# Causal attention ahead of two MLP blocks on one core: PSUM banks as separate tiles, and another order of scores, transposes and copies

## Chip, core and metric

One core of a Trainium2 chip (trn2) runs the whole program in one launch. The metric is the device time of that launch in microseconds (us). Times inside an execution come from a hardware profile of one execution: start and duration of each instruction on each engine, counted from the start of the span. The engines are TensorE (PE in the profile; its weight loads are listed apart as PEld), VectorE (DVE), ScalarE (ACT), GpSimd (POOL) and SyncE (SP), which here only issues DMAs.

## What is computed

Two batches, 12 heads, 448 positions, head size 64, all fp32. The causal attention output, laid out as 896 rows of 768, goes through two MLP blocks one after the other (768 to 2048 to 768, with a parametric ReLU in the first and a clipped square in the second).

```python
scores = scale * np.matmul(q, k.transpose(0, 1, 3, 2))
scores = np.where(mask, -1000000000.0, scores)          # causal
scores = scores - np.max(scores, axis=-1, keepdims=True)
attn = np.exp(scores)
attn = attn / (np.sum(attn, axis=-1, keepdims=True) + 1e-09)
x = np.matmul(attn, v)                                  # then (B*S, H*D)
h = x @ w_in;  g = np.maximum(h, 0) + alpha * np.minimum(h, 0);  x = g @ w_out
h = x @ w2_in; g = where(h >= 1, h, where(h <= -1, 0, (h + 1)**2 / 4)); out = g @ w2_out
```

## The kernel before

The program has two stages. The attention stage (lines 463 to 526) loops over 12 pairs of heads, `for p in range(NP + 2)`. The MLP stage (`run_layer`, lines 280 to 311) then runs four layers of matmuls of 128x448 columns back to back.

A pair holds two heads j = 0 and 1 on the two halves of 64 partitions. The 448 query rows are three row tiles i = 0, 1, 2 of 128 rows and a rest of 64 rows (i = NQ = 3); a row tile needs keys up to its own end, so the score tiles have 128, 256, 384 and 448 columns. The rests of the two heads are done together in one matmul with a block-diagonal `qdiag`.

Three pairs are in work at once. In turn p of the loop, in program order: `scores` of pair p for row tiles 0 and 1, then the rest (lines 493, 494); `expo` (ScalarE); `attnv` of pair p-2 and its evacuation `high` on ScalarE (lines 497 to 499); `spare(0)`, which from turn 3 on issues one step of the splitting of an MLP weight; `scores` for row tile 2; `transp` of pair p-1 (lines 504, 511, 512); `low` on VectorE; `expo` for row tile 2; `norm` of pair p (GpSimd and one reciprocal on VectorE); the DMA loads for later pairs, issued by SyncE. The last two turns have no new pair and take in the first MLP matmuls (`fill`) instead.

Each engine takes its instructions in that program order; the schedule is fixed by hand, and the framework adds the waits. It orders accesses per tile of a pool: an engine that writes a PSUM tile waits for readers of the same tile on another engine, and a reader waits for the last write into the tile ahead of it.

The PSUM has eight banks of 512 fp32 columns. Before, tag `s` is one tile of two banks (head j in bank j), `rest` and `o` one bank each, and tag `t` two buffers of two banks.

In `scores` (lines 366 to 394) every score matmul is followed at once by its masked reduction on VectorE (line 390), which writes the masked scores to SBUF and the row minimum of the negated scores to `stat`. In `transp` (lines 415 to 440) 64x64 blocks of the probabilities go through TensorE transposes into a `t` tile, partition half h of the rows into bank h; then line 440 copies them to `pt` in SBUF, head 0 by ScalarE and head 1 by VectorE, each copy reading both banks. There are three calls a pair: row tile 0 with the rest, row tile 1, row tile 2. In `attnv` (lines 442 to 450) eight products, four key chunks c by two heads j, add up in the bank `o`, over columns c*128 to 448; the heads fill the two column halves of the array. An fp32 matmul appears as two instructions in the profile, a transpose as one.

`evac_out` (lines 220 to 229) ends the program; the last two output tiles come from one two-bank `t` tile.

Of the kernel before, what the change touches and what calls it, by code (L numbers as in the profile page):

```python
# [22 lines left out]
def attention_moe_moe_kernel(ctx: ExitStack, tc: tile.TileContext, qk, v, w1, w2, w3, w4, alpha, out):  # L23
# [8 lines left out]
    nc = tc.nc  # L32
# [205 lines left out]
    def new_banks():  # L238

        def one(pool, tag):  # L240
            return pool.tile([128, 512], F32, tag=tag, name="ps")

        def two(pool, tag):
            both = pool.tile([128, 1024], F32, tag=tag, name="ps")
            return both[:, :512], both[:, 512:]

        while True:
            yield from two(ps_s, "s")
            yield one(ps_o, "rest")
            yield one(ps_o, "o")  # L250
            yield from two(ps_t, "t")
            yield from two(ps_t, "t")
# [61 lines left out]
    class Attention:  # L314
# [51 lines left out]
        def scores(self, p, tiles):  # L366
# [4 lines left out]
            if NQ in tiles:  # L371
                both = self.ps_o.tile([128, 512], F32, tag="rest", name="rest_ps")
            else:
                both = self.ps_s.tile([128, 1024], F32, tag="s", name="s_ps")
            off = 0
            for i in tiles:
                for n, (e, col) in enumerate(self.rows(p, i)):
                    w = e.shape[1]
                    ps = both[:, n * 512 + off:n * 512 + off + w]
                    if i == NQ:  # L380
                        nc.tensor.matmul(ps, lhsT=self.qdiag[p % 3], rhs=t[:, 1, :], start=True, stop=True)  # L381
                        m = mask_rest
                    else:
# [4 lines left out]
                        m = mask[:, REST - w:]  # L388

                    nc.vector.tensor_tensor_reduce(  # L390
                        out=e, in0=ps, in1=m, scale=-SCALE, scalar=3.0e38, op0=ALU.add, op1=ALU.min,
                        accum_out=self.st[p][:, 0, col:col + 1],
                    )
                off += w
# [10 lines left out]
        def norm(self, p):  # L405
# [3 lines left out]
            for i in (0, NQ, 1, 2):  # L409
# [5 lines left out]
        def transp(self, p, tiles):  # L415

            ps = self.ps_t.tile([128, 1024], F32, tag="t", name="t_ps").rearrange("p (h n) -> p h n", h=2)
            if 0 in tiles:
                self.pt[p] = self.ap.tile([Q, 2, NC, S], F32, tag="pt", name="pt", bufs=2)
            pt, off, copies = self.pt[p], 0, []  # L420
            for i in tiles:
                n = NC if i == NQ else i + 1
                rows = self.rows(p, i)
                dst = ps[:, :, off:off + len(rows) * n * D].rearrange("p h (j c q) -> p h j c q", c=n, q=D)
                off += len(rows) * n * D
                for c in range(n):
                    for j, (e, _) in enumerate(rows):
                        e = self.prest[p % 3] if i == NQ else e
                        for h in range(2):
                            g = slice(h * D, (h + 1) * D)  # L430
                            nc.tensor.transpose(dst[:, h, j, c, :], e[g, c * Q:(c + 1) * Q], ident[g, g])  # L431
                for j, copy in enumerate((nc.scalar.copy, nc.vector.tensor_copy)):
# [23 lines left out]
    with tc.manual_schedule():  # L456
# [6 lines left out]
        with ExitStack() as pa:  # L463
# [18 lines left out]
            for p in range(NP + 2):  # L482
# [20 lines left out]
                if mid:  # L503
                    at.transp(p - 1, (0, NQ))
# [74 lines left out]
```

## Time and profile before

| | us |
|---|---|
| median of 3 runs | 684.62 (677.09 to 686.32) |
| the profiled execution, its own time | 675.95 |
| its span in the profile | 674.1 |
| TensorE busy (matmuls) | 617.2 |
| VectorE busy | 424.7 |
| ScalarE busy | 248.0 |
| GpSimd busy | 132.6 |
| mean granted TensorE clock, share of 2.4 GHz | 0.932 |

The busy times are sums over both stages and must be read stage by stage. The attention stage runs from about 9 us to about 209 us, the MLP stage from there to the end. "Idle before" and the arrow in a row tell how long the engine stood still ahead of the group and what released it. Matmul ends are modelled, and a matmul's duration includes its latency, so rows that follow each other at once overlap a little.

### The profile page before, as it was taken

What the parts mean: (1) busy time and instruction counts of PE and PEld (TensorE: products, weight loads), DVE (VectorE), ACT (ScalarE), POOL (GpSimd) and SP (SyncE); (2) the same over time, 40 slices, a digit from 0 to 9 for tenths busy, and PEclk for the clock granted to TensorE, in tenths of its full rate; (3) what the DMA queues carried; (4) which work ended last, traced back from release to release, by engine and by line L of the source; (5) the groups of instructions that cost most, each with busy time, mean ns of one, the idle gap of its engine ahead of it and who ended that gap; (6) DMA issues with size and microseconds to landing.
All of it is one profiled execution on the core that took longest, in us unless ns stands there. A gap on an engine that the chain in (4) does not pass through costs nothing.

```text
span 674.1 us, 8430 instructions
## 1 busy us (share of the span) xinstructions
PE 617.2 (92%) x3057; PEld 505.8 (75%) x3057; DVE 424.7 (63%) x797; ACT 248.0 (37%) x509; POOL 132.6 (20%) x179
## 2 busy tenths in 40 slices
PE   7776677777789999999999999999999999999997
PEld 3333333333367999999999999999999999999996
DVE  1333333433336889889886666688888986666650
ACT  2344333434322433433333232345556453322220
POOL 1222322222220333343300000024334331000000
PEclk9996776777779999999999999999999999999999
DMA  4421111310002333332344333423323224534430
GB/s 125 142 69 50 53 45 44 90 44 0 1 1 94 97 137 94 99 121 63 109 142 125 93 100 113 163 94 128 107 95 108 96 63 124 153 122 131 141 93 27
DMA packets 25673, 62.29 MB, mean 92 GB/s; under 512 B 5280, under 2 KB 13984, under 8 KB 25632
## 3 DMA queue, kind: packets, MB, share of 16 engines
q1 hardware_dynamic: 23760, 60.15, 28.8%
q10 hardware_dynamic: 1872, 1.61, 0.7%
q8 instruction: 24, 0.39, 0.2%
q14 instruction: 17, 0.14, 0.1%
HBM read 58.99 MB, written 2.75 MB: 92 GB/s over the span
## 4 chain that ended last, share of the span: by engine, by line
PE 89%; DVE 6%; ACT 3%; issue 1%; POOL 0%; ACTq 0%; DVEq 0%; POOLq 0%
PE ps L262 69%; PE s_ps L385 9%; PE o_ps L447 5%; PE rest_ps L381 3%; DVE pexp L390 3%; DVE pt L440 2%; ACT pt L440 2%; PE t_ps L431 2%; ACT pexp L400 2%; PE warm_ps L72 1%; DVE stat L408 0%; DVE stat L390 0%; DVE w_split L153 0%; DVE w_f L147 0%; ACT w_split L150 0%
## 5 line engine op out<-in xcount | busy, mean ns | idle before, releaser
L262 PE MATMUL ps<-x,w_split 128*128 128x448 f32 x1152 | 235.2, 366 | 0.7 <-DVE w_split L153 0.7
L262 PE MATMUL ps<-g,w_split 128*128 128x448 f32 x1152 | 234.1, 365 | 0.9 <-DVE o_sb L226 0.9
L262 PEld LDWEIGHTS ps<-g,w_split 128*128 128x128 f32 x1152 | 216.3, 188 | 18.3 <-DVE o_sb L226 1.3
L262 PEld LDWEIGHTS ps<-x,w_split 128*128 128x128 f32 x1152 | 216.2, 188 | 18.4 <-DVE w_split L153 1.1
L177 POOL TENSOR_TENSOR g<-act_g,g 128x448 fp32r<-128x448 f32 x64 | 85.5, 1336 | 275.3 <-ACT g L176 275.2
L150 ACT CAST w_split<-w_f 128x512 fp32r<-128x512 f32 (+1 forms) x80 | 56.6, 707 | 127.4 <-DVE w_f L147 96.7
L385 PE MATMUL s_ps<-qk_raw 64*128 64x128 f32 (+2 forms) x144 | 70.6, 584 | 33.3 <-DVE stat L390 33.3
L153 DVE TENSOR_TENSOR w_split<-w_f,w_split 128x512 fp32r<-128x512 f32 (+1 forms) x80 | 66.0, 825 | 49.2 <-ACT w_split L150 49.0
L390 DVE CUSTOM_DVE_ANT_0 pexp<-s_ps,mask 128x128 f32<-128x128 f32 (+2 forms) x72 | 30.0, 417 | 94.3 <-PE s_ps L385 94.3
L385 PEld LDWEIGHTS s_ps<-qk_raw 64*128 64x128 f32 x144 | 30.7, 265 | 61.7 <-DVE stat L390 57.9
L176 ACT CAST g<-act_g 128x448 fp32r<-128x448 f32 x64 | 36.2, 565 | 76.5 <-DVE act_g L189 62.8
L147 DVE SCALAR_TENSOR_TENSOR w_f<-w_raw,w_f 128x512 uint32<-128x512 uint32 (+1 forms) x80 | 63.4, 793 | 1.4
L141 DVE SCALAR_TENSOR_TENSOR w_f<-w_raw,w_f 128x512 uint32<-128x512 uint32 (+1 forms) x80 | 63.4, 793 | 1.4
L129 DVE TENSOR_SCALAR w_f<-w_f 128x512 f32<-128x512 f32 (+1 forms) x80 | 58.2, 727 | 9.5 <-ACT w_f L113 9.3
L113 ACT ACTIVATE w_f<-w_raw 128x512 f32<-128x512 f32 (+1 forms) x80 | 61.2, 765 | 1.3 <-DMA w_raw<-w 1.3
L400 ACT ACTIVATE pexp<-pexp,stat 128x128 f32<-128x128 f32 (+2 forms) x72 | 36.4, 506 | 57.3 <-DVE stat L390 57.3
L447 PEld LDWEIGHTS o_ps<-pt,v 128*64 128x64 f32 x192 | 18.5, 192 | 30.8 <-issue 14.3
L135 DVE TENSOR_SCALAR w_f<-w_f 128x512 uint32<-128x512 uint32 (+1 forms) x80 | 38.0, 475 | 1.4
L447 PE MATMUL o_ps<-pt,v 128*64 128x320 f32 (+3 forms) x192 | 37.2, 544 | 0.6 <-ACT pt L440 0.6
L411 POOL TENSOR_SCALAR pexp<-pexp,stat 128x128 f32<-128x128 f32 (+2 forms) x72 | 33.8, 486 | 13.6 <-DVE stat L390 9.6
L431 PE MATMUL t_ps<-ident,pexp 64*128 64x64 f32 x288 | 21.2, 241 | 15.5 <-DVE pt L440 15.5
L201 ACT ACTIVATE act_t<-act_t,half 128x448 f32<-128x448 f32 x32 | 21.5, 672 | 37.7 <-DVE act_t L200 37.7
(43 smaller groups left out, 286.3 us busy)
## 6 DMA issues: line engine op xcount, KB each, us to landing
w_raw<-w SPq DMA_DIRECT2D x32, 768.0 KB, 4.3
w_raw<-w SPq DMA_DIRECT2D x48, 512.0 KB, 3.7
qk_raw<-qk SPq DMA_DIRECT2D x11, 448.0 KB, 3.6
out<-o_sb SPq DMA_DIRECT2D x12, 112.0 KB, 1.7
out<-o_sb ACTq DMA_DIRECT2D x12, 112.0 KB, 1.7
v<-v SPq DMA_DIRECT2D x12, 56.0 KB, 2.5
v<-v SPq DMA_DIRECT2D x12, 48.0 KB, 2.0
v<-v SPq DMA_DIRECT2D x12, 40.0 KB, 1.9
```

What stands on the lines that cost most here:

```text
L113: nc.scalar.activation(out=f32(w), in_=f32(hi), func=AF.Abs)
L129: nc.vector.tensor_scalar(out=f32(w), in0=f32(w), scalar1=HI_MIN, scalar2=HI_MAX, op0=ALU.max, op1=ALU.min)
L141: nc.vector.scalar_tensor_tensor(out=w, in0=hi, scalar=0xC0000000, in1=w, op0=ALU.bitwise_and, op1=ALU.bitwise_or)
L147: nc.vector.scalar_tensor_tensor(out=w, in0=lo, scalar=29, in1=w, op0=ALU.logical_shift_right, op1=ALU.bitwise_or)
L150: nc.scalar.copy(s[:, 0, :n], f32(w))
L153: nc.vector.tensor_sub(s[:, 1, :n], f32(w), f32(s[:, 0, :n]))
L177: nc.gpsimd.tensor_sub(t[:, 1, :], g, f32(t[:, 0, :]))
L262: nc.tensor.matmul(ps[b][:, :S], lhsT=ws[:, part, k * 128:(k + 1) * 128], rhs=src[b, kk][:, xp, :], start=first and part == 0 and xp == 0, ...
L385: nc.tensor.matmul(ps, lhsT=t[h, 0, i * Q:(i + 1) * Q], rhs=t[h, 1, :w], start=True, stop=True)
L390: nc.vector.tensor_tensor_reduce(out=e, in0=ps, in1=m, scale=-SCALE, scalar=3.0e38, op0=ALU.add, op1=ALU.min, accum_out=self.st[p][:, 0, c ...
L400: nc.scalar.activation(out=e, in_=e, func=AF.Exp, bias=st[:, 0, col:col + 1], scale=-1.0, accum_out=st[:, 1, col:col + 1],)
L447: nc.tensor.matmul(ps[j * D:(j + 1) * D, c * Q:S], lhsT=vraw[:, c, j, :], rhs=pt[:, j, c, c * Q:S], start=c == 0, stop=c == NC - 1,)
```

## The change

PSUM is cut into single-bank tiles: `s0`, `s1` (head 0 and 1 of the row tiles), `s2` (the rest), `o`, and two buffers each of `t0` and `t1`. `new_banks` hands the MLP stage the same eight banks one by one. `scores` issues all matmuls of a call first and all reductions after them. `transp` puts partition half h into the tile `t{h}`; for row tiles ScalarE copies all of half 0 and VectorE all of half 1 (both heads in one copy), into separate ranges of `pt`; the rest gets its own tile `pt_rest`, and both its copies are VectorE's. The calls are now (0, 1), (NQ), (2). `attnv` does the 384 columns of the row tiles in six products, chunk by head, whose moving operand and output are two interleaved sets of runs of 64 columns, and the rest's 64 columns in eight products of their own. `norm` scales row tile 1 ahead of the rest.

```diff
--- before.py
+++ after.py
@@ -237,19 +237,10 @@
 
     def new_banks():
 
-        def one(pool, tag):
-            return pool.tile([128, 512], F32, tag=tag, name="ps")
-
-        def two(pool, tag):
-            both = pool.tile([128, 1024], F32, tag=tag, name="ps")
-            return both[:, :512], both[:, 512:]
-
+        pools = (ps_s, "s0"), (ps_s, "s1"), (ps_s, "s2"), (ps_o, "o"), (ps_t, "t0"), (ps_t, "t1"), (ps_t, "t0"), (ps_t, "t1")
         while True:
-            yield from two(ps_s, "s")
-            yield one(ps_o, "rest")
-            yield one(ps_o, "o")
-            yield from two(ps_t, "t")
-            yield from two(ps_t, "t")
+            for pool, tag in pools:
+                yield pool.tile([128, 512], F32, tag=tag, name="ps")
 
     def new_tile():
         return next(banks)
@@ -369,29 +360,30 @@
                 self.st[p] = self.ap.tile([Q, 2, 2 * NQ + 1], F32, tag="stat", name="stat", bufs=4)
             t = self.raw[p]
             if NQ in tiles:
-                both = self.ps_o.tile([128, 512], F32, tag="rest", name="rest_ps")
+                banks = [self.ps_s.tile([128, 512], F32, tag="s2", name="rest_ps")]
             else:
-                both = self.ps_s.tile([128, 1024], F32, tag="s", name="s_ps")
-            off = 0
+                banks = [self.ps_s.tile([128, 512], F32, tag=f"s{j}", name=f"s{j}_ps") for j in range(2)]
+            off, todo = 0, []
             for i in tiles:
                 for n, (e, col) in enumerate(self.rows(p, i)):
                     w = e.shape[1]
-                    ps = both[:, n * 512 + off:n * 512 + off + w]
+                    ps = banks[n][:, off:off + w]
                     if i == NQ:
                         nc.tensor.matmul(ps, lhsT=self.qdiag[p % 3], rhs=t[:, 1, :], start=True, stop=True)
-                        m = mask_rest
+                        todo.append((e, ps, mask_rest, col))
                     else:
                         h = slice(n * D, (n + 1) * D)
                         nc.tensor.matmul(
                             ps, lhsT=t[h, 0, i * Q:(i + 1) * Q], rhs=t[h, 1, :w], start=True, stop=True
                         )
-                        m = mask[:, REST - w:]
-
-                    nc.vector.tensor_tensor_reduce(
-                        out=e, in0=ps, in1=m, scale=-SCALE, scalar=3.0e38, op0=ALU.add, op1=ALU.min,
-                        accum_out=self.st[p][:, 0, col:col + 1],
-                    )
+                        todo.append((e, ps, mask[:, REST - w:], col))
                 off += w
+
+            for e, ps, m, col in todo:
+                nc.vector.tensor_tensor_reduce(
+                    out=e, in0=ps, in1=m, scale=-SCALE, scalar=3.0e38, op0=ALU.add, op1=ALU.min,
+                    accum_out=self.st[p][:, 0, col:col + 1],
+                )
 
         def expo(self, p, tiles):
             st = self.st[p]
@@ -406,7 +398,7 @@
             sums = self.st[p][:, 1]
             nc.gpsimd.tensor_scalar_add(sums, sums, 1e-9)
             nc.vector.reciprocal(sums, sums)
-            for i in (0, NQ, 1, 2):
+            for i in (0, 1, NQ, 2):
                 for e, col in self.rows(p, i):
                     nc.gpsimd.tensor_scalar(
                         out=e, in0=e, scalar1=sums[:, col:col + 1], scalar2=1.0, op0=ALU.mult, op1=ALU.mult
@@ -414,38 +406,53 @@
 
         def transp(self, p, tiles):
 
-            ps = self.ps_t.tile([128, 1024], F32, tag="t", name="t_ps").rearrange("p (h n) -> p h n", h=2)
+
+            ps = [self.ps_t.tile([128, 512], F32, tag=f"t{h}", name=f"t{h}_ps") for h in range(2)]
             if 0 in tiles:
-                self.pt[p] = self.ap.tile([Q, 2, NC, S], F32, tag="pt", name="pt", bufs=2)
-            pt, off, copies = self.pt[p], 0, []
+
+                self.pt[p] = (
+                    self.ap.tile([Q, 2, 2, NQ, NQ * D], F32, tag="pt", name="pt", bufs=2),
+                    self.ap.tile([Q, 2, NC, D], F32, tag="pt_rest", name="pt_rest", bufs=2),
+                )
+            (pt, pt_rest), off, copies = self.pt[p], 0, []
             for i in tiles:
                 n = NC if i == NQ else i + 1
                 rows = self.rows(p, i)
-                dst = ps[:, :, off:off + len(rows) * n * D].rearrange("p h (j c q) -> p h j c q", c=n, q=D)
+                dst = [
+                    t[:, off:off + len(rows) * n * D].rearrange("p (j c q) -> p j c q", c=n, q=D) for t in ps
+                ]
                 off += len(rows) * n * D
                 for c in range(n):
                     for j, (e, _) in enumerate(rows):
                         e = self.prest[p % 3] if i == NQ else e
                         for h in range(2):
                             g = slice(h * D, (h + 1) * D)
-                            nc.tensor.transpose(dst[:, h, j, c, :], e[g, c * Q:(c + 1) * Q], ident[g, g])
-                for j, copy in enumerate((nc.scalar.copy, nc.vector.tensor_copy)):
-                    to = pt[:, j, :n, i * Q:]
-                    if i == NQ:
-
-                        copies.append((copy, to, dst[:, j, 0]))
-                    else:
-                        copies.append((copy, to[:, :, :Q].rearrange("p c (h q) -> p h c q", h=2), dst[:, :, j]))
+                            nc.tensor.transpose(dst[h][:, j, c, :], e[g, c * Q:(c + 1) * Q], ident[g, g])
+                if i == NQ:
+
+                    for h in range(2):
+                        copies.append((nc.vector.tensor_copy, pt_rest[:, h], dst[h][:, 0]))
+                else:
+                    for h, copy in enumerate((nc.scalar.copy, nc.vector.tensor_copy)):
+                        copies.append((copy, pt[:, h, :, :n, i * D:(i + 1) * D], dst[h]))
             for copy, to, src in copies:
                 copy(to, src)
 
         def attnv(self, p):
-            ps = self.o[p] = self.ps_o.tile([2 * D, 512], F32, tag="o", name="o_ps")
-            pt, vraw = self.pt[p], self.vraw[p % 5]
+            o = self.o[p] = self.ps_o.tile([2 * D, 512], F32, tag="o", name="o_ps")
+            (pt, pt_rest), vraw = self.pt[p], self.vraw[p % 5]
+            for c in range(NQ):
+                for j in range(2):
+                    nc.tensor.matmul(
+                        o[j * D:(j + 1) * D, c * Q:REST].rearrange("p (i h q) -> p h i q", h=2, q=D),
+                        lhsT=vraw[:, c, j, :],
+                        rhs=pt[:, :, j, c, c * D:].rearrange("p h (i q) -> p h i q", q=D),
+                        start=c == 0, stop=c == NQ - 1,
+                    )
             for c in range(NC):
                 for j in range(2):
                     nc.tensor.matmul(
-                        ps[j * D:(j + 1) * D, c * Q:S], lhsT=vraw[:, c, j, :], rhs=pt[:, j, c, c * Q:S],
+                        o[j * D:(j + 1) * D, REST:S], lhsT=vraw[:, c, j, :], rhs=pt_rest[:, j, c, :],
                         start=c == 0, stop=c == NC - 1,
                     )
 
@@ -501,14 +508,14 @@
                 if new:
                     at.scores(p, (2,))
                 if mid:
-                    at.transp(p - 1, (0, NQ))
+                    at.transp(p - 1, (0, 1))
                 if old:
                     low()
                 if new:
                     at.expo(p, (2,))
                 spare(2)
                 if mid:
-                    at.transp(p - 1, (1,))
+                    at.transp(p - 1, (NQ,))
                     at.transp(p - 1, (2,))
                 if new:
                     at.norm(p)
```

## Rows read from the trace of the kernel before

**Rows 1.** The page, granted TensorE clock in 40 slices, tenths of full speed
```profile
PEclk9996776777779999999999999999999999999999
```

**Rows 2.** Busy time by stretch: window, length, engines' busy us, PEclk, DMA share, GB/s
```profile
90.00:120.00 30.00, 21.71 (x121) 11.60 (x118) 11.03 (x39) 10.90 (x36) 7.20 (x16) 0.67 0.17 49
120.00:150.00 30.00, 21.32 (x124) 10.52 (x122) 12.12 (x42) 12.65 (x39) 7.20 (x16) 0.73 0.25 75
...
280.00:300.00 20.00, 20.00 (x101) 18.53 (x100) 18.38 (x26) 6.24 (x11) 6.65 (x6) 1.00 0.31 112
```

**Rows 3.** Timeline, TensorE, first group of turns 0, 1, 3, 12: start, us, what
```profile
9.41 0.79 PE L385 MATMUL s_ps<-qk_raw 64*128 64x128 f32 x2
...
21.19 0.79 PE L385 MATMUL s_ps<-qk_raw 64*128 64x128 f32 x2 [0.66 <-DVE stat L390]
...
50.26 0.44 PE L385 MATMUL s_ps<-qk_raw 64*128 64x128 f32 x2
...
193.04 4.27 PE L447 MATMUL o_ps<-pt,v 128*64 128x448 f32 x16 [0.57 <-ACT pt L440]
```

**Rows 4.** Timeline, TensorE's matmuls of turn 6, without the transposes
```profile
97.02 0.44 PE L385 MATMUL s_ps<-qk_raw 64*128 64x128 f32 x2
98.78 0.79 PE L385 MATMUL s_ps<-qk_raw 64*128 64x128 f32 x2 [1.32 <-DVE stat L390]
99.97 1.22 PE L385 MATMUL s_ps<-qk_raw 64*128 64x256 f32 x2 [0.39 <-DVE stat L390]
101.71 1.22 PE L385 MATMUL s_ps<-qk_raw 64*128 64x256 f32 x2 [0.53 <-DVE stat L390]
102.86 1.86 PE L381 MATMUL rest_ps<-qk_raw,qdiag 128*128 128x448 f32 x2
104.65 3.68 PE L447 MATMUL o_ps<-pt,v 128*64 128x448 f32 x16
108.26 1.19 PE L385 MATMUL s_ps<-qk_raw 64*128 64x384 f32 x2
110.11 0.59 PE L385 MATMUL s_ps<-qk_raw 64*128 64x384 f32 x1 [0.66 <-DVE stat L390]
...
113.74 0.74 PE L385 MATMUL s_ps<-qk_raw 64*128 64x128 f32 x2
```

**Rows 5.** Timeline, turn 6: first reduction of row tile 2, copies, last transposes
```profile
109.48 0.56 DVE L390 CUSTOM_DVE_ANT_0 pexp<-s_ps,mask 128x384 f32<-128x384 f32 x1 [3.23 <-PE s_ps L385]
...
111.47 0.27 ACT L440 COPY pt<-t_ps 128x128 f32<-128x128 f32 x1 [2.56 <-PE t_ps L431]
...
111.77 0.29 DVE L440 COPY pt<-t_ps 128x128 f32<-128x128 f32 x1 [0.15 <-ACT pt L440]
112.10 0.37 ACT L440 COPY pt<-t_ps 128x256 f32<-128x256 f32 x1 [0.36 <-DVE pt L440]
...
112.50 0.42 DVE L440 COPY pt<-t_ps 128x256 f32<-128x256 f32 x1 [0.44 <-ACT pt L440]
...
113.07 0.90 PE L431 MATMUL t_ps<-ident,pexp 64*128 64x64 f32 x12 [1.44 <-DVE pt L440]
```

**Rows 6.** Busy time by stretch, single microseconds of turn 6
```profile
105.00:106.00 1.00, 1.00 (x4) 0.24 (x2) 1.00 (x3) 0.58 (x2) 0.00 (x0) 0.50 0.00 0
109.00:110.00 1.00, 0.45 (x2) 0.00 (x0) 0.52 (x2) 0.00 (x0) 0.00 (x0) 1.00 0.00 0
112.00:113.00 1.00, 0.00 (x0) 0.00 (x0) 0.56 (x3) 0.90 (x4) 0.00 (x0) 0.63 0.89 151
```

**Rows 7.** Timeline, weight loads of attention times values, turns 6 and 7
```profile
107.58 0.56 PEld L447 LDWEIGHTS o_ps<-pt,v 128*64 128x64 f32 x4
...
123.37 0.30 PEld L447 LDWEIGHTS o_ps<-pt,v 128*64 128x64 f32 x4
```

**Rows 8.** Timeline, first score matmul of row tile 2 in turn 7
```profile
123.74 0.91 PE L385 MATMUL s_ps<-qk_raw 64*128 64x384 f32 x2
```

**Rows 9.** Timeline, the last matmuls of the program
```profile
667.87 2.74 PE L262 MATMUL ps<-g,w_split 128*128 128x448 f32 x12 [0.90 <-DVE o_sb L226]
```

## The prediction, written before the changed kernel was run

> **What bounds the kernel now.** I read the clock line of the page first. It is full from about the thirteenth slice on and lower before [rows 1]: the program has two halves with different limits. The table by stretch says what they are. From 280 to 300 us TensorE is busy all 20 us at full clock: the MLP stage is bound by its matmuls, and the change leaves those as they are. In the attention stage TensorE is busy 21.3 to 21.7 of 30 us at a mean clock of 0.67 to 0.73, and VectorE, ScalarE and GpSimd 12.1, 12.7 and 7.2 us at the most [rows 2]. No engine is full there, so waits set the pace. Turns 3 to 11 take 193.04 - 50.26 = 142.78 us, or 15.86 us each; turns 0 to 2 take 50.26 - 9.41 = 40.85 us [rows 3].
>
> Then TensorE's timeline of one turn, cut into four parts [rows 4]:
> - a, the four score matmuls of row tiles 0 and 1: 97.02 to 102.86, 5.84 us. Three of them wait for VectorE's reduction of the one before (1.32, 0.39, 0.53 us of standing still, and each pays its latency anew).
> - b, the rest: to 104.65, 1.79 us.
> - c, attention times values: to 108.26, 3.61 us.
> - d, row tile 2 and the transposes: to 113.74, 5.48 us, with 0.66 us of waiting for a reduction. The last transposes start after 1.44 us of waiting for a VectorE copy that ends a chain in which ScalarE and VectorE take turns, four copies one after the other from 111.47 on [rows 5].
>
> **The change, part by part, for one turn.** The reader should carry two columns, as TensorE ran at both 1.2 and 2.4 GHz in this stage.
>
> Part a. The heads have their own banks and the reductions come behind the four matmuls, so nothing stands between them. At 1.2 GHz a 256-column matmul holds up the next for 102.86 - 101.71 = 1.15 us, a 128-column one 0.72 us (its 0.79 us less the 0.07 us by which the others overlap) [rows 4]. One after another: 2 x (0.72 + 1.15) = 3.7 us. The two heads use different halves of the array's rows and now different banks; wholly at once they take 1.9 us. No score matmuls of two heads run side by side in this trace, so both ends stay; I take 1.9, since in turn 6 the second score matmul of row tile 2 is split in the trace by transposes that start inside it [rows 4]. At 2.4 GHz 128 columns took 0.44 us [rows 4] and 384 took 0.91 us [rows 8]; 256 in the middle is 0.68, so 1.1 us at once and 2.2 us in turn. The page "TensorEngine Tiling (Array Packing)" of the Trainium skill, section Key Properties, says that different tiles load and multiply in parallel: by it part a is 1.9 and 1.1 us, the lower ends. Its next property, that a change of tiling mode drains the engine, is in the rows already, since b and c change mode now as before.
>
> Part b stays: 1.79 us, or 1.0 us at 2.4 GHz (by 0.44 / 0.79 = 0.56).
>
> Part c keeps its 1024 columns for each head, 3.61 us or 2.0 us, but has 14 products where it had 8, 28 instructions for 16. Four weight loads took 0.56 us at the low clock and 0.30 us at the high one [rows 7], at most 0.14 and 0.075 us each. Twelve more cost nothing if they hide behind the streams, at the most 1.7 and 0.9 us; I take half, 0.8 and 0.45 us. So c is 4.4 or 2.45 us, the one part that gets dearer.
>
> Part d. The second matmul of row tile 2 follows the first. The 20 transposes of the first two calls take 20 x 0.67 / 12 = 1.1 us (12 of them held up the next matmul for 113.74 - 113.07 = 0.67 us) and hide behind VectorE's work. The last call still waits: its buffer is free when VectorE has copied the first call's, behind both reductions of row tile 2. That is the first matmul (1.19 or 0.91 us) + 2 x 0.56 + 0.29 + 0.42, or 3.0 and 2.75 us, and then 0.67 us of transposes [rows 4, 5, 8]: d is 3.7 or 3.4 us. If the two 384-column matmuls run in turn at 1.2 GHz, TensorE itself is later: 2 x 1.19 + 1.1 + 0.67 = 4.2 us.
>
> Added up, a turn takes 11.8 us at 1.2 GHz and 8.0 us at 2.4 GHz with the heads side by side, and 14.1 and 9.1 us without.
>
> What is late next? VectorE and ScalarE were busy at most 12.12 and 12.65 of 30 us [rows 2], 6.4 and 6.7 us a turn; VectorE gains one 256-column copy (0.42 us), ScalarE loses one (0.37 us) [rows 5]. 6.8 and 6.3 us still fit into 8.0, GpSimd's 3.8 us too, so the new order of `norm` costs nothing as long as GpSimd has that slack. DMA goes from at most 0.25 of its time [rows 2] to at most twice that. New waits: the first reduction now also waits for the third matmul, as both write `s0`, and the other reductions queue behind it. Only row tile 2's matmuls need them, after b and c (3.4 to 6.2 us), and four reductions of at most 0.56 us [rows 5] are done by then. The rest's two copies are VectorE's, between `low` and the last call's copy; behind them are the reciprocal and the next turn's reductions, which have part a as slack. With 6.8 us of work in a turn of 8.0, VectorE is the next bound.
>
> The clock decides between the columns. TensorE was at 1.2 GHz while it was already multiplying without a break (0.50 at 105 us, from 102.86 on), at 2.4 GHz at 109 us, and fell again in the microsecond from 112 in which it did nothing [rows 6]. After the change a, b, c and the start of d follow one another without a wait, and the only stop left, before the last transposes, is about 1 us. So I expect more time at the high clock than the 34 to 46% that means of 0.67 to 0.73 make, but drops in d on some turns. I put 9.4 us a turn, which is some 63% of the way from 11.8 to 8.0.
>
> **The sum.** Turns 3 to 11: 9 x (15.86 - 9.4) = 58.1 us. Turns 0 to 2, at the low clock: turn 0 has neither c nor transposes, 1.9 + 1.8 + 1.2 + 0.9 = 5.8 us; turn 1 no c, 11.8 - 4.4 = 7.4; turn 2 11.1; together 24.3 for 40.85, 16.5 us saved. The last two turns are filled with MLP matmuls; I leave them. At the end the 0.90 us in which the last product waited for the copy out of its two-bank tile go [rows 9]. Together 75.5 us off the profiled execution's 675.95: 600 us. The median of the runs shown (684.62) lies 1.3% above that execution; half of such an excess makes 604.
>
> **The rivals.**
> - The clock stays at 1.2 GHz (the low clock held until 108 us although TensorE was busy; against it, the rise came in the end): 11.8 us a turn, 9 x 4.06 + 15.8 + 0.9 = 53 us, 623 us.
> - The heads' matmuls run in turn, not at once: at the same clock 14.1 - 0.63 x 5.0 = 10.95 us a turn; 9 x 4.9 + 10.2 + 0.9 = 55 us, 621 us. With the low clock as well, 650 us.
> - The six larger products of c, which now read and write runs of 64 columns at a stride, stream slower. They carry 768 of 1024 columns, 2.7 us at the low clock and 1.5 at the high, say 1.95. At half the rate 12 x 1.95 = 23 us come back: 624 us. Every product in the trace writes one unbroken run, so only the rate's two ends, unchanged and halved, can be set. The page "PSUM — Partial Sum Buffer" of the Trainium skill, section Specifications, says that any non-contiguous access pattern slows matmuls significantly; by it this rival is the case. No run here shows it yet.
> - The change doesn't do what it says: tiles of one bank still make readers and writers wait as before. Then only the twelve weight loads are left, 12 x 0.6 = 7 us more: 683 us.
> - Slower than before: the stride of c again, at a price that eats everything. It decides from (75.5 + 13.5) / 12 = 7.4 us a turn, the 768 columns at 4.8 times their time. Copies in this trace that read PSUM in runs of 64 took 0.37 to 0.42 us for 256 columns [rows 5], nothing of that size; but those are not matmuls.
>
> **How the numbers follow.** Chances: the forecast 0.61, low clock 0.15, heads in turn 0.10, half rate of c 0.08, waits remain 0.04, slower 0.02. The forecast's own range is the all-high and the all-low column, 583 to 623 us. The range 580 to 636 takes in the next three and half a per cent more for runs above the profiled one. A measurement of this kernel tells about 2% from no change: faster by more than that 0.94, within it 0.04 (the waits remain), slower by more 0.02.
>
> **What would show it.** In TensorE's timeline four score matmuls within 1.1 to 1.9 us and no wait for `stat` between them; ScalarE's and VectorE's copies of a call starting together; turns of 8.0 to 11.8 us; a mean clock near 0.8 in the stage; the weight loads of c at 28 a turn in 2.45 to 4.4 us. I am wrong if VectorE shows no idle time in a turn, if c passes 5 us, or if the clock reads 0.5 throughout.

## The result, and the profile after

| | before | after |
|---|---|---|
| median of 4 runs on one chip, us | 680.86 (675.37 to 686.32) | 569.44 (567.31 to 578.95) |
| the profiled execution, its own time, us | 675.95 | 569.33 |
| its span in the profile, us | 674.1 | 567.4 |
| mean granted TensorE clock | 0.932 | 0.996 |

The time after is 0.838 of the time before (95% interval 0.827 to 0.848). 604 us were predicted, with a range of 580 to 636: the direction was right, the gain came out larger than even the range's lower end allowed. In some executions all MLP matmuls run about 2% slower (98 or 99 in the 20 us from 280 on, where 100 or 101 is usual), which adds 7 to 10 us to the total; the profiled executions of the kernel before with its waits filled (both versions) and of the first copies-first version were such, so of these the turns are compared and not the total.

The page of after: the granted clock in 40 slices, the share of each engine in the chain that ended last, and the last layers' matmuls (busy us, mean ns, idle time before them).
```profile
PEclk9999998999999999999999999999999999999999
...
PE 95%; DVE 3%; issue 1%; POOL 1%; ACT 0%; ACTq 0%; POOLq 0%
...
L253 PE MATMUL ps<-g,w_split 128*128 128x448 f32 x1152 | 233.8, 365 | 0.0
```
The row of sixes and sevens in the clock line of before [rows 1] is gone. The chain that sets the end is now TensorE's own work for 95% of the span. The last layers wait for nothing; before, their one wait was that of [rows 9].

The timeline of after, TensorE: where turns 0, 1, 3 and 12 start, with one later group of turn 1 (start, us, what, wait before it).
```profile
9.41 1.65 PE L376 MATMUL s_ps<-qk_raw 64*128 64x128 f32 x8
...
14.84 1.40 PE L376 MATMUL s_ps<-qk_raw 64*128 64x128 f32 x8 [0.66 <-DVE stat L383]
17.57 0.93 PE L376 MATMUL s_ps<-qk_raw 64*128 64x384 f32 x3 [0.38 <-DVE stat L383]
...
27.38 0.90 PE L376 MATMUL s_ps<-qk_raw 64*128 64x128 f32 x8
...
89.20 2.83 PE L446 MATMUL o_ps<-pt,v 128*64 128x384 f32 x12 [1.10 <-DVE stat L400]
```
Set against [rows 3] these starts say where the time went:

| stretch | before, us | after, us | gain | predicted |
|---|---|---|---|---|
| turns 0 to 2 | 50.26 - 9.41 = 40.85 | 27.38 - 9.41 = 17.97 | 22.9 | 16.5 |
| turns 3 to 11 | 193.04 - 50.26 = 142.78 | 89.20 - 27.38 = 61.82 | 81.0 | 58.1 |
| turn 12 to the end of the span | 674.1 - 193.04 = 481.06 | 567.4 - 89.20 = 478.20 | 2.9 | 0.9 |

The three gains add up to 106.7 us, the difference of the spans. Turns 3 to 10 take 6.72 us each and turn 11 takes 8.02, a mean of 6.87 for 15.86 before.

One turn of after in TensorE's timeline, with the copies of row tile 2's wait.
```profile
61.01 0.90 PE L376 MATMUL s_ps<-qk_raw 64*128 64x128 f32 x8
61.84 1.02 PE L372 MATMUL rest_ps<-qk_raw,qdiag 128*128 128x448 f32 x2
62.78 1.52 PE L446 MATMUL o_ps<-pt,v 128*64 128x384 f32 x12
64.13 0.63 PE L454 MATMUL o_ps<-pt_rest,v 128*64 128x64 f32 x16
64.69 0.92 PE L376 MATMUL s_ps<-qk_raw 64*128 64x384 f32 x4
...
65.44 0.54 PE L430 MATMUL t_ps<-ident,pexp 64*128 64x64 f32 x12
65.81 0.42 PE L430 MATMUL t_ps<-ident,prest 64*128 64x64 f32 x8
...
66.70 0.24 PE L430 MATMUL t_ps<-ident,pexp 64*128 64x64 f32 x1 [0.47 <-ACT pt L439]
...
67.36 0.55 PE L430 MATMUL t_ps<-ident,pexp 64*128 64x64 f32 x11 [0.42 <-DVE pt L439]
67.73 0.90 PE L376 MATMUL s_ps<-qk_raw 64*128 64x128 f32 x8
```
The first row is all four score matmuls of row tiles 0 and 1 in one group, without a wait. In the parts of the prediction this turn is a 0.83, b 0.94, c 1.91 and d 3.04 us; before, a alone took 5.84 [rows 4]. TensorE's only stops are the two ahead of the last transposes, 0.47 + 0.42 = 0.89 us.

Busy time of the same turn and of turn 11 (window, length, TensorE, its weight loads, VectorE, ScalarE, GpSimd, granted clock, DMA share, GB/s):
```profile
61.01:67.73 6.72, 5.83 (x81) 3.75 (x78) 5.94 (x24) 5.16 (x19) 4.31 (x8) 1.00 0.70 231
...
81.18:89.20 8.02, 6.02 (x82) 3.84 (x77) 6.85 (x28) 5.70 (x20) 4.15 (x9) 0.98 0.00 0
```
VectorE is busy 5.94 of 6.72 us, where 12.12 of 30 was the most before [rows 2]. Turn 11 lasts longer because TensorE stands still 1.10 us at its end (the 89.20 row above), for VectorE's reciprocal of line 400.

### The profile page after: what moved, and what is told of

It reads as the page before. It is cut to its first block, busy times and chain, and to the rows that moved or that the text cites. A ratio compares the mean times of both kernels' runs of the same rounds, so it can differ in the third digit from the quotient of the medians.

```text
span 567.4 us, 8740 instructions
## 1 busy us (share of the span) xinstructions
PE 550.1 (97%) x3201; PEld 482.7 (85%) x3201; DVE 420.9 (74%) x809; ACT 237.8 (42%) x497; POOL 136.1 (24%) x179
## 3 DMA queue, kind: packets, MB, share of 16 engines
HBM read 58.99 MB, written 2.75 MB: 109 GB/s over the span
## 4 chain that ended last, share of the span: by engine, by line
PE 95%; DVE 3%; issue 1%; POOL 1%; ACT 0%; ACTq 0%; POOLq 0%
PE ps L253 82%; PE s_ps L376 3%; PE o_ps L446 3%; PE rest_ps L372 2%; DVE pexp L383 2%; PE warm_ps L72 1%; PE t_ps L430 1%; DVE pt L439 1%; PE o_ps L454 1%; POOL pexp L403 0%; ACT pexp L392 0%; POOL prest L403 0%; DVE x L216 0%; DVE stat L383 0%; DVE zero L69 0%
## 5 line engine op out<-in xcount | busy, mean ns | idle before, releaser
L253 PEld LDWEIGHTS ps<-g,w_split 128*128 128x128 f32 x1152 | 216.4, 188 | 17.1
L383 DVE CUSTOM_DVE_ANT_0 pexp<-s_ps,mask 128x128 f32<-128x128 f32 (+2 forms) x72 | 26.2, 412 | 22.6 <-PE s_ps L376 22.5
L226 DVE COPY o_sb<-ps 128x224 f32<-128x224 f32 x12 | 4.7, 392 | 29.9 <-ACT o_sb L226 29.9
L430 PEld LDWEIGHTS t_ps<-ident,pexp 64*128 64x128 f32 x288 | 13.5, 138 | 15.2 <-issue 8.4
L430 PE MATMUL t_ps<-ident,pexp 64*128 64x64 f32 x288 | 16.1, 226 | 9.3 <-ACT pt L439 4.9
L376 PE MATMUL s_ps<-qk_raw 64*128 64x128 f32 (+2 forms) x144 | 23.8, 425 | 1.0 <-DVE stat L383 1.0
L446 PEld LDWEIGHTS o_ps<-pt,v 128*64 128x64 f32 x144 | 9.9, 143 | 14.5 <-issue 11.1
```

The source lines that it names most:

```text
L253: nc.tensor.matmul(ps[b][:, :S], lhsT=ws[:, part, k * 128:(k + 1) * 128], rhs=src[b, kk][:, xp, :], start=first and part == 0 and xp == 0, ...
L376: nc.tensor.matmul(ps, lhsT=t[h, 0, i * Q:(i + 1) * Q], rhs=t[h, 1, :w], start=True, stop=True)
L383: nc.vector.tensor_tensor_reduce(out=e, in0=ps, in1=m, scale=-SCALE, scalar=3.0e38, op0=ALU.add, op1=ALU.min, accum_out=self.st[p][:, 0, c ...
```

## The experiments

They separate three things that the change does together: it takes waits out of the score matmuls, it lets the heads run side by side, and by both it keeps TensorE's clock up. The kernel before, run beside them, took 675.55 us with the first four, and 676 us in the median with the others.

### The clock alone: the kernel before, its waits filled

```diff
+    def dummies(n):
+        if n:
+            ps = ps_o.tile([128, 512], F32, tag="rest", name="dummy_ps")
+            for _ in range(n):
+                nc.tensor.matmul(ps, lhsT=zero[0][:, :128], rhs=zero[0], start=True, stop=True)
...
                         m = mask[:, REST - w:]
+                        dummies({(0, 0): 5, (0, 1): 1, (1, 0): 2, (2, 0): 3}.get((i, n), 0))
...
+                    if new:
+                        dummies(5)
                     at.transp(p - 1, (2,))
```


> The kernel before, with matmuls of zeros issued into TensorE's waits of the attention stage (5, 1 and 2 behind the first three score matmuls of a turn, 3 behind the first of row tile 2, 5 ahead of the last transposes), into the bank of the rest, which nobody reads then; all waits and tiles stay as before. Theory 'waits first, clock second': with TensorE at 2.4 GHz throughout, the four parts of a turn are 4.4 + 1.0 + 1.95 + 5.0 = 12.4 us instead of 15.86, so the clock alone is worth some 3.5 of the 9.0 us that a turn lost between the two kernels; about 638 us. Rival 'the clock is most of it': turns under 9 us, about 600 us. Rival 'the low clock comes with the waits whatever fills them': turns of 15.9 us or more, 676 us or more.

658.74 us. Busy time of one turn, and two groups of it in TensorE's timeline:
```profile
67.97:80.45 12.48, 12.39 (x85) 6.96 (x81) 5.87 (x21) 5.96 (x20) 3.62 (x8) 1.00 0.20 61
```
```profile
68.34 1.43 PE L80 MATMUL dummy_ps<-zero 128*128 128x512 f32 x5
...
70.61 0.70 PE L393 MATMUL s_ps<-qk_raw 64*128 64x256 f32 x2
```
The granted clock is 1.00 and the turn takes 12.48 us, although TensorE multiplies 16 more matmuls in it. So of the 9.0 us that a turn gained (15.86 to 6.87), at least 3.4 are to be had from the clock with every wait left where it was. The rest, at most 5.6, needs the waits gone or the heads side by side. The total missed the forecast of 638 us, in part because turns 0 to 2 got longer, 46.1 us: there the zeros ran while durations were still those of 1.2 GHz. That clock held although TensorE did not stop once in turn 1:
```profile
24.71:43.10 18.39, 18.39 (x63) 9.82 (x63) 4.44 (x18) 5.74 (x19) 3.88 (x9) 1.00 0.25 70
```
```profile
32.76 1.86 PE L389 MATMUL rest_ps<-qk_raw,qdiag 128*128 128x448 f32 x2
```
The duration tells the clock here: these two instructions take 1.86 us, and 1.02 us at the high clock. Why the 1.00 of the first row does not tell it is said in the last section.

To leave the early turns alone, the same from turn 3 on (both calls with `if p >= 3`):

> The kernel before with matmuls of zeros in TensorE's waits, now from turn 3 on only, where the clock has risen at times; all waits stay. Theory 'the clock is worth 3.4 of the 9 us a turn': turns 3 to 11 take 12.5 us, turns 0 to 2 the 40.9 us of the kernel before, 675.5 - 9 x 3.4 = 645 us. Rival 'the matmuls of zeros cost as much as the clock gives back': 655 us or more.

658.49 us. Turns 4 to 10 take about 12.5 us each (they start at 67.73, 80.21, 92.69), as in the kernel above; turn 3 takes 17.1, still at the low clock. The reading by turns holds from turn 4 on; the forecast of the total, 645 us, does not.

### One half of the change at a time

Scores as after (one bank for each head, reductions behind the matmuls), transposes, copies, `attnv` and `norm` as before (the diff is against after):

```diff
-            ps = [self.ps_t.tile([128, 512], F32, tag=f"t{h}", name=f"t{h}_ps") for h in range(2)]
+            ps = self.ps_t.tile([128, 1024], F32, tag="t", name="t_ps").rearrange("p (h n) -> p h n", h=2)
...
-                    at.transp(p - 1, (0, 1))
+                    at.transp(p - 1, (0, NQ))
...
-                    at.transp(p - 1, (NQ,))
+                    at.transp(p - 1, (1,))
```


> The changed scores (three one-bank tiles, reductions behind the matmuls) with the transposes, copies, order of calls and attention times values of before. Theory 'the scores carry the change, and a dense stretch keeps the clock': full clock, part a under 1 us, the stop ahead of the last transposes longer by about 0.7 us because the copies still take turns; turns of about 7.5 us, some 578 us. Part c of before, at full clock for the first time, about 1.9 us, which shows what the strided products and the twelve more weight loads cost. Rival 'both halves are needed to hold the clock': mixed clock, turns of 9 us or more, 600 us or more.

The other half: scores as before, transposes, copies, `attnv` and `norm` as after (again against after):

```diff
-                banks = [self.ps_s.tile([128, 512], F32, tag=f"s{j}", name=f"s{j}_ps") for j in range(2)]
+                both = self.ps_s.tile([128, 1024], F32, tag="s", name="s_ps")
...
+                    nc.vector.tensor_tensor_reduce(...)
-            for e, ps, m, col in todo:
-                nc.vector.tensor_tensor_reduce(...)
```

> The scores of before (one two-bank tile, a reduction behind each matmul) with the changed transposes, copies and attention times values. Theory 'the scores carry the change': part a keeps its three waits and the low clock, part d loses 1.5 to 2 us; turns of about 14 us, some 655 us. Rival 'the transposes carry it': turns under 11 us at a full clock, 620 us or less.

Scores alone 584.34 us, transposes alone 659.07. Beside them the kernel before took 675.55; after, timed later on another chip, 567.27. The gains are 91.2 and 16.5 us, together 107.7 for the 108.3 of both: the halves add, with one execution of each. The scores-only kernel is 6 us over its forecast: of its turns 3 to 10 six take 7.3 to 7.4 us and two 8.9, at a granted clock of 0.81, and turn 2 was at a lowered clock too. The stop ahead of the last transposes, 1.67 to 1.84 us long, is in every turn from turn 2 on; ahead of turns 6 and 7 it was the same, and only turn 6 lost the clock:
```profile
53.24 0.59 PE L426 MATMUL t_ps<-ident,pexp 64*128 64x64 f32 x12 [1.67 <-DVE pt L435]
...
62.14 0.59 PE L426 MATMUL t_ps<-ident,pexp 64*128 64x64 f32 x12 [1.67 <-DVE pt L435]
```
```profile
53.63:62.53 8.90, 7.23 (x69) 3.70 (x66) 6.00 (x21) 5.52 (x20) 4.30 (x8) 0.81 0.30 80
62.53:69.89 7.36, 5.60 (x70) 3.37 (x66) 6.09 (x21) 6.04 (x21) 4.30 (x8) 1.00 0.45 119
```
With the transposes alone, TensorE waits as in [rows 4]: a turn of 13.97 us (64.29 to 78.26) still has the three stops of part a, of which this is one:
```profile
66.64 1.22 PE L378 MATMUL s_ps<-qk_raw 64*128 64x256 f32 x2 [0.39 <-DVE stat L383]
```
With the scores alone, part c in its old layout runs at the high clock, which no turn of before had shown whole:
```profile
71.67 1.95 PE L442 MATMUL o_ps<-pt,v 128*64 128x448 f32 x16
...
73.55 0.92 PE L379 MATMUL s_ps<-qk_raw 64*128 64x384 f32 x4
```
That is 73.55 - 71.67 = 1.88 us for 8 unbroken products. After needs 1.91 us for 14 products that write and read runs of 64 columns. Stride and extra weight loads together cost 0.03 us.

### Where the reductions stand, and what a stop costs beyond itself

After, with each reduction issued right behind its matmul, so that `s0` and `s1` have readers between two writes:

```diff
                         todo.append((e, ps, mask[:, REST - w:], col))
+                    e, ps, m, col = todo.pop()
+                    nc.vector.tensor_tensor_reduce(...)
                 off += w
-            for e, ps, m, col in todo:
-                nc.vector.tensor_tensor_reduce(...)
```


> The changed kernel with each reduction issued right behind its score matmul again, the tiles staying apart. Theory 'banks and order are both needed': the third matmul, which writes the bank of the first, waits for the first reduction, and that one for VectorE to finish the copies of the turn before; part a grows from 0.83 to about 2.2 us, turns of 8.1 us, some 585 us. Rival 'separate banks are enough': turns of 6.7 us, 569 us.

600.31 us, 15 more than the forecast of 585. Two successive turns, and the wait that came back:
```profile
63.14:72.99 9.85, 7.95 (x82) 4.44 (x78) 6.07 (x24) 5.49 (x19) 3.62 (x8) 0.83 0.26 69
72.99:81.20 8.21, 6.31 (x82) 4.04 (x78) 6.17 (x24) 6.20 (x20) 4.32 (x8) 1.00 0.48 144
```
```profile
64.61 0.91 PE L376 MATMUL s_ps<-qk_raw 64*128 64x256 f32 x4 [1.01 <-DVE stat L381]
```
At full clock the turn is 1.49 us longer than in after; the wait is 1.01 of it, and most of the rest is that the first pair of matmuls runs out, 0.47 us, before the second pair starts. In the other turn the granted clock is 0.83 and it takes 1.64 us more. To see whether the clock makes that difference, the same kernel with four zero matmuls in that wait from turn 2 on:

```diff
+                    if (i, n) == (0, 1) and p >= 2:
+                        dummies(4)
                     e, ps, m, col = todo.pop()
```


> The kernel with each reduction right behind its score matmul and separate banks, and from turn 2 on four matmuls of zeros, into the bank of the rest, in the 1.0 us that TensorE waits ahead of the third score matmul; waits and order are otherwise those of that kernel, which took 600.31 us with turns of 8.21 and 9.85 us. Theory 'the slow turns are the clock's': it stays full, all turns take 8.2 us, some 584 us, although TensorE has more to do. Rival 'the slow turns have another cause': turns of 8.2 and 9.9 us again, 600 us or more.

588.18 us. The same stretch of the run:
```profile
57.45:65.65 8.20, 7.30 (x85) 4.66 (x82) 6.16 (x24) 5.48 (x19) 4.32 (x8) 1.00 0.28 80
65.65:73.86 8.21, 7.31 (x85) 4.66 (x82) 6.17 (x24) 6.21 (x20) 4.32 (x8) 1.00 0.45 141
```
TensorE does 1 us more in each turn, each of turns 3 to 10 takes 8.2 us, and the program is 12 us faster. The long turns were the clock's doing.

After, with one buffer each for `t0` and `t1` (two other single banks go to the MLP):

```diff
-        pools = (ps_s, "s0"), (ps_s, "s1"), (ps_s, "s2"), (ps_o, "o"), (ps_t, "t0"), (ps_t, "t1"), (ps_t, "t0"), (ps_t, "t1")
+        pools = (ps_s, "s0"), (ps_s, "s1"), (ps_s, "s2"), (ps_o, "o"), (ps_t, "t0"), (ps_t, "t1"), (ps_t, "t2"), (ps_t, "t3")
...
-            for n, b in (("s", 1), ("t", 2), ("o", 1))
+            for n, b in (("s", 1), ("t", 1), ("o", 1))
```


> The changed kernel with one buffer each for the transposes' two tiles (the MLP stage gets two tiles of its own for the banks set free, so its rotation stays). The second call of transposes waits for the copies of the first, the third for those of the second. Theory 'the clock has room': TensorE stands still about 1.7 us and 1.0 us in part d, the clock stays full, turns of about 8.3 us, some 588 us. Rival 'the change only just holds the clock': it falls in most turns, 9.5 us or more a turn, 600 us or more.

596.12 us, for a forecast of 588 with a full clock. Two successive turns, and the stops of the first:
```profile
59.67:67.67 8.00, 6.28 (x80) 3.96 (x78) 6.13 (x22) 5.26 (x18) 4.30 (x8) 1.00 0.31 91
67.67:77.27 9.60, 7.88 (x80) 4.37 (x78) 6.29 (x22) 6.09 (x19) 4.30 (x8) 0.82 0.49 145
```
```profile
65.40 0.24 PE L430 MATMUL t_ps<-ident,prest 64*128 64x64 f32 x1 [0.72 <-ACT pt L439]
66.06 0.43 PE L430 MATMUL t_ps<-ident,prest 64*128 64x64 f32 x7 [0.42 <-DVE pt L439]
...
67.07 0.77 PE L430 MATMUL t_ps<-ident,pexp 64*128 64x64 f32 x11 [0.58 <-DVE pt_rest L439]
```
The stops are 1.72 us a turn instead of 0.89, all of them waits for a copy. At full clock the turn is 1.28 us longer than in after, in the other turn the clock reads 0.82 and 1.6 us come on top. Of turns 3 to 10 this kernel and the reduce-at-once kernel each lose the clock in five (turns of 9.6 us or more), the scores-only kernel in two; after, whose stops are shorter, loses it in none.

### Head by head

After, with the score matmuls issued 128 and 256 columns of head 0, then the same of head 1, to put the heads in turn:

```diff
-            for i in tiles:
-                for n, (e, col) in enumerate(self.rows(p, i)):
+            for n in range(len(self.rows(p, tiles[0]))):
+                off = 0
+                for i in tiles:
+                    e, col = self.rows(p, i)[n]
...
+            todo.sort(key=lambda x: x[3])
```

> The changed kernel with the score matmuls of row tiles 0 and 1 issued head by head (head 0 tile 0, head 0 tile 1, head 1 tile 0, head 1 tile 1) instead of tile by tile; reductions in the same order as before. Theory 'the two heads run side by side on the halves of the array's rows': now two matmuls of the same half follow each other and most of the overlap goes; part a grows from 0.83 to about 1.3 us, and being on the chain this makes turns of about 7.2 us, some 575 us. Rival 'no overlap, the short part a is the clock alone': unchanged, 6.7 us a turn, 569 us.

567.6 us, turns of 6.75: no change. That is what the rival without overlap forecast, so the time does not tell the two apart; the trace does. The score matmuls that run between 67.6 and 67.65 us, and those between 67.6 and 67.75, by form (count, ns shortest, median and longest, first and last start):
```profile
L379 PE MATMUL s_ps<-qk_raw x4: 272/298/349, 67.4 to 67.6; 64*128 64x128 f32 x4
...
L379 PE MATMUL s_ps<-qk_raw x6: 272/337/378, 67.4 to 67.7; 64*128 64x128 f32 x4, 64*128 64x256 f32 x2
```
All four 128-column instructions, two for each head, have started by 67.6 us and the first two of 256 columns start after them, though head 1's 128 columns come after head 0's 256 in the program. By these records a matmul on the other half of the rows went ahead of its place. So this order did not take the side by side away, and the run doesn't measure what it is worth. What side by side is worth shows elsewhere: the 256-column products of both heads took 0.91 us in the reduce-at-once kernel (the 64.61 row), that of one head alone took 0.70 in the filled kernel (the 70.61 row), both at full clock. In the filled kernel one head's matmuls hold up what follows for 0.37 us (128 columns, 67.97 to 68.34) and 0.63 us (256 columns, 70.61 to 71.24); both heads in turn would take some 2.0 us, where part a of after takes 0.83. By this estimate the side by side is worth some 1.2 us a turn in part a alone.

### After again, and a faster version

After itself again, on another chip:

> The changed kernel unaltered, beside the others on the same chip: 569 us, turns of 6.7 us.

567.27 us in the median of 4 (567.11 to 569.27), 0.838 of before (0.831 to 0.844).

If VectorE's queue sets d, putting its copies ahead of the second reduction of row tile 2 should free TensorE sooner. `norm` goes ahead of the last call's copies as well. With `late=1`, `scores` hands back its last reduction instead of issuing it (left out below).

```diff
...
-                    at.scores(p, (2,))
+                    rest_of_2 = at.scores(p, (2,), late=1)
                 if mid:
                     at.transp(p - 1, (0, 1))
+                if new:
+                    for op in rest_of_2:
+                        op()
...
-                    at.transp(p - 1, (2,))
                 if new:
                     at.norm(p)
+                if mid:
+                    at.transp(p - 1, (2,))
```


> The changed kernel with VectorE's copies of the first transposes ahead of the second reduction of row tile 2, and the normalization of the new pair (the reciprocal on VectorE) ahead of the last call's copies. Theory 'the chain of a turn runs through VectorE's two reductions and two copies': the last transposes start up to 0.47 us earlier, until GpSimd's scaling of row tile 2 is what they wait for; turns of 6.3 to 6.4 us, about 565 us. Rival 'VectorE is full': no change, 569 us.

565.19 us in the median of 5, 0.834 (0.826 to 0.842). The same kernel again:

> The version with VectorE's copies ahead of the second reduction, once more: 565 us, turns of 6.3 to 6.7 us.

565.34 us in the median of 4 (564.93 to 565.49), 0.835 (0.828 to 0.841). Turns 3 to 11 take 59.74 us (26.53 to 86.27) for 61.83 in the repeat of after (26.66 to 88.49). The 2.1 us agree with the difference of the medians, 567.27 - 565.34 = 1.9. Of turns 3 to 10 five are as short as expected, 6.24 to 6.32 us; turns 3, 7 and 9 take 6.7 to 6.8. The last transposes of a short and of a long turn:
```profile
64.51 0.74 PE L434 MATMUL t_ps<-ident,pexp 64*128 64x64 f32 x12 [0.47 <-ACT pt L443]
...
71.31 0.76 PE L434 MATMUL t_ps<-ident,pexp 64*128 64x64 f32 x12 [0.96 <-ACT pt L443]
```
The chain of the long turn (start, us, engine, what) says why:
```profile
67.06 1.86 ACT pexp L396 x8
68.92 0.65 ACT prest L396 x2
69.57 0.42 ACT x L213
69.99 0.15 ACT w_f L113
```
VectorE has left the chain and ScalarE has taken its place: its copy stands behind the exponentials, `high` and an operation of the weight splitting. Only the three long turns have such an operation there (0.90 us at 31.37, 0.83 at 56.97, 0.90 at 69.89). This is the fastest version that ran, by 0.3 to 0.4% over after.

## Why the prediction was too small

The profiled execution was forecast at 600.4 us and took 569.3, 31 us less. Four steps of the sum account for it: the clock with 9 x 1.4 = 12.6 us, the price of a turn at full clock with 9 x 1.28 = 11.5 less the 1.3 of the longer last turn, the first three turns with 6.3, and the end with 2.0. With the clock alone put right the sum is 588 us, with the full-clock turn alone 589, both within the range; with both it is 576, below it. The 3.6 us added for runs above the profiled one did not come either: the median is 569.44.

**The clock: the step that failed.** "9.4 us a turn, which is some 63% of the way from 11.8 to 8.0" took the clock as mixed, with drops in d on some turns. It reads 1.00 in every turn from 3 to 10. The mechanism was named rightly as far as it goes (the clock fell before in the microsecond in which TensorE did nothing [rows 6]; filling the wait of the reduce-at-once kernel brought its clock back), but the stop was put at about 1 us and then charged as if it cost the clock; it is two stops of 0.47 and 0.42 us, and it does not. The reduce-at-once and one-buffer kernels show that this was near: with a wait of 1.01 us more, or 1.72 us of stops in place of 0.89, turns at a clock of 0.82 to 0.83 appear and cost 1.6 us each. Their turns of 9.85 and 9.60 us are near the 9.4 that I forecast for after. But the length of one stop does not decide it: the 1.67 us of the scores-only kernel cost the clock in two turns of eight, and the 1.10 us at the end of turn 11 cost it in the profiled execution of after (part c of turn 12 takes 2.83 us for its twelve larger instructions) and not in the repeat (1.51 us, at 88.49).

**The full-clock turn: mechanism right, three terms too dear.** 8.0 us were written, 6.72 measured.
- a, 1.1 us written, 0.83 measured, and b, 1.0 and 0.94. The 128- and 256-column prices came from groups that stood alone [rows 4], and so carried latency that a row of matmuls pays once.
- c, 2.45 and 1.91 us. Half the price of twelve weight loads (0.45 us) was charged; they hide, as the 1.88 us of the old layout beside 1.91 shows. The rest is the ratio 0.56 from 128-column matmuls: the old c took 3.61 at the low clock [rows 4] and 1.88 at the high one, 0.52.
- d, 3.4 and 3.04 us. The wait was right nearly to the tenth: 2.75 us written from the first score matmul to the last transposes, 67.36 - 64.69 = 2.67 measured. The last transposes were charged 0.67 us, a row of the low clock [rows 5]; they take 67.73 - 67.36 = 0.37.

DMA, put at no more than half of its time, is busy 0.70 of this turn; none of TensorE's waits in turns 3 to 10 is put down to it.

The chain of waits of after in this turn (start, us, engine, what) is the chain that part d wrote down: first matmul, two reductions, VectorE's copies, transposes.
```profile
64.76 0.90 PE s_ps L376 x4
65.66 0.54 DVE pexp L383
66.20 0.01 DVE stat L383
66.21 0.47 DVE pexp L383
66.68 0.01 DVE stat L383
66.69 0.55 DVE pt L439 x2
67.23 0.14 issue
67.36 0.55 PE t_ps L430 x11
67.92 0.71 PE s_ps L376 x8
```
"VectorE is the next bound" holds here too, and the copies-first version, which took VectorE out of this chain, gained what little ScalarE left.

**The first three turns.** All three were summed at the low clock, turn 2 with 11.1 us for which no working is shown. The four score matmuls take 1.65 us in turn 0, 1.40 in turn 1 and 0.90 from turn 3 on; within turn 1 the 384-column group is already at 0.93. The clock had risen by then. That TensorE is no longer stopped for long cannot be the whole reason, since the kernel filled from turn 0 kept the low clock through nearly all of a turn 1 without a stop; the cause of the early rise stays open.

**The end.** The 0.90 us of [rows 9] went as written. Another 1.7 us are in turns 12 and 13, which were left unchanged in the sum: from the start of turn 12 to the start of the unbroken MLP matmuls 15.84 us before and 14.14 after. Part c of turn 12 took 4.20 and now 3.41 us (1.91 in the repeat, where the clock held), and a wait of 0.75 us for a weight split is gone. The remaining 0.3 us I did not trace.

**The rivals.**
- Low clock, 623 us: false, by the clock line.
- Heads in turn, 621 us: false. The first matmuls of both heads start 0.03 us apart in after, at 61.01 us, and two heads cost 0.91 us where one costs 0.70. This agrees with the Trainium skill, page "TensorEngine Tiling (Array Packing)", section Key Properties, on tiles that multiply in parallel.
- Strided products of c at half rate, 624 us, and its extreme, slower than before: false, 1.91 beside 1.88 us. The Trainium skill's page "PSUM — Partial Sum Buffer", section Specifications (TRN2), has any non-contiguous pattern slow matmuls significantly; for fp32 runs of 64 columns the measurement says otherwise, and it decides.
- Waits remain, 683 us: false; the scores-only kernel shows that the separate banks with the late reductions are worth 91 us by themselves.

Of the signs that were to tell me wrong none came: VectorE stands idle 0.78 us a turn, c is 1.91 us, the clock full. They lacked one for the faster side. But four signs that were to show the forecast did not come either: the four score matmuls (0.90 us for 1.1 to 1.9), the turn (6.72 for 8.0 to 11.8), c (1.91 for 2.45 to 4.4) and the clock of the stage (1.00 for near 0.8).

What stays open is what the side by side of the heads is worth in the whole, since no kernel here took it away, what lets the clock of after rise so early, and why the reduce-at-once, the one-buffer and the scores-only kernel lose the clock in some turns and keep it in others of the same work.

## What to carry to other kernels

When waits are taken out of a stage that runs at a mixed clock, sum a turn at full clock first, list the stops left in it, and give the case that the clock holds a chance and a lower end of its own instead of a mean of the two levels: here 0.8 us of stops a turn more or less, with the clock that it cost in five turns, was the difference between 596 and 567 us. Take prices at full clock from groups in which the same instruction repeats, not from one that stands alone. Reductions queued between two writes of one PSUM tile are worth moving behind all writes even where the reading engine is half idle: here that and a bank for each head were five sixths of the gain.

## What the runs showed that I had not expected

- A kernel got faster by doing useless work: four zero matmuls a turn in a wait took the reduce-at-once kernel from 600.31 to 588.18 us, and sixteen took a turn of before from 15.86 to 12.48.
- By the trace's records a matmul on the other half of the array's rows starts ahead of its place in the program: in the head-by-head kernel all four instructions of 128 columns start before the first of 256.
- At the start of the span the clock line reads 9 while the durations are those of the low clock: the eight instructions of 128 and 256 columns at 9.41 us take 1.65 us, 0.90 later. The packed trace has no clock record ahead of 13.8 us in after, 42.5 us in the kernel filled from turn 0 and 44.0 us in before, and a stretch without one is shown as full. In the first turns durations are to be trusted, not that line, and the mean clocks in the tables (0.932 and 0.996) are too high by that stretch.
